# Attention and two layers on one core: reciprocals transposed and multiplied into a float32 output that layer 1 splits, and layer 2's mask and cubic constant made by ScalarE

## The chip, the core and the metric

The kernel runs on one core of a Trainium2 chip. TensorE (PE in the profile, its weight loads PEld) multiplies matrices into PSUM; VectorE (DVE), ScalarE (ACT) and GpSimd (POOL) work element by element; SyncE's queue (SP) issues the transfers. Each engine runs its own instructions in order and waits for others by semaphores. The metric is the time of one execution on the chip in microseconds, the median of several runs.

## The reference

Attention over 4 batches of 8 heads, 576 positions of 64 numbers, then two layers with different activations on its output of 2304 tokens by 512:

```python
q_rot, k_rot = rotate(q), rotate(k)
scores = (1 / sqrt(64)) * (q_rot @ k_rot.T)
attn = exp(scores - max(scores))
attn = attn / (sum(attn) + 1e-9)
x = attn @ v                                  # to 2304 x 512
h = x @ w_in                                  # layer 1, 512 x 2048
x = where(h > 0, h, exp(min(h, 0)) - 1) @ w_out
h = x @ w_in2                                 # layer 2
out = (h - tanh(h)) @ w_out2
```

## The kernel before

**Attention.** The heads come in 16 pairs (`p`). A pair has nine items (line 180): blocks `u` of 128 query rows, `u` = 0 to 3 once for each head (`h` = 0, 1), and a last item with the remaining 64 rows of both heads (`h` = None). The main loop goes over the 144 items and for each item `i` writes out work of several items, so that the engines overlap: the maximum of item `i` (`emit_max`, DVE), copies from PSUM that were left over (`flush`), the scores of item `i+1` (`emit_s`, PE), the exponentials of `i` with their row sums `den` (`emit_exp`, ACT), the normalisation of `i-1` (`emit_norm`: 1e-9 is added and the reciprocal taken on DVE, and POOL multiplies the exponentials `a` by it), the transposes of item `i-D` with `D = 4` (`emit_t`, PE, into `pt` and, for the 64 columns left of both heads, `pr`), and parts of the product with `v` (`emit_pv`, PE, into `o`). `flush` copies `pt` and `pr` to `aT` and `aTr`, two in five on DVE and three on ACT. `manual_schedule` keeps the order in which this is written on every engine.

The output `o` stays in PSUM until ACT has cast it to the float32r tile `xh` and, an item later, DVE has subtracted that from it into `xl` (lines 265 to 276): the layers multiply with such split numbers, high part and rest. Rotation of the next pair's q and k (`prep`, five steps at the items that `sched` names) multiplies with the tables `tabs` (line 143, mostly POOL), adds (line 145, DVE), casts (line 148, ACT) and subtracts (line 153, DVE); `place` then sends the parts to `qa`, `qb` and `k` through SP's queue. The scale 1/8 comes in with the last two steps. One weight block in two pairs is converted (`conv_w`, on ACT, DVE and POOL).

**Layers.** A step is one block of 128 of the 2048 inner columns for one tile of 384 tokens: 4 groups of 4 blocks by 6 tiles, 96 steps a layer. Per step PE makes `h` from 12 matmuls (`emit_f1`, line 441) and, four steps later (`LAG`), multiplies the activations `g` into `y` (`emit_f2`, line 498 in layer 1, 500 in layer 2). Four PSUM buffers hold `y`; a layer 2 tile needs three, and after its fourth step they are added to `acc` by DVE (line 517) or, in the first group, copied by ACT (line 515). In layer 2 `emit_act` and `emit_dve` (lines 453 to 476) make `h - tanh(h)`: for large `h` as a subtraction, and where `u = h*h` is under 0.09 by a polynomial `(w + G1) * h * u`, taken over through a mask.

Of the kernel before, what the change touches and what calls it, by code (L numbers as in the profile page):

```python
# [24 lines left out]
def attention_elu_tanhshrink(ctx: ExitStack, tc: tile.TileContext, qk, v, w1i, w1o, w2i, w2o, tab, out):  # L25
# [76 lines left out]
    with ExitStack() as actx:  # L102
# [17 lines left out]
        def load_qk(p, x):  # L120
            if p == 1 and x == 0:
                t = p3.tile([128, 2, S], F32, tag="a", name="t0")
            else:
                t = (p1, p2)[x].tile([128, 2, S], F32, tag=f"t{x}", name=f"t{x}")
# [8 lines left out]
        def prep(p, x, i):  # L133
            t = t_t[p, x]
            mul = SCALE if p > 0 and x == 0 else 1.0
            if i < 2:
# [4 lines left out]
                else:  # L141
                    eng = nc.vector if p < 2 and i == 1 else nc.gpsimd
                    eng.tensor_tensor(out=t[:, i, :], in0=t[:, i, :], in1=tabs[:, i, :], op=ALU.mult)  # L143
# [470 lines left out]
```

## Time and profile before

| | us |
|---|---|
| median of the runs (lowest, highest) | 1145.89 (1145.56, 1146.97) |
| the profiled execution | 1145.03 |
| its span in the profile | 1143.2 |
| PE busy | 1100.3 (96%) |
| DVE busy | 844.6 (74%) |
| POOL busy | 655.9 (57%) |
| ACT busy | 612.9 (54%) |

The busy times are averages over stages with different limits, so the table by stretch has to be read beside them. A busy PE isn't PE at its peak, since matmuls overlap and their ends are modelled. A row of the groups gives the line, engine, operation, what is written from what, shapes and count, then the busy time and the mean of one, then the engine's idle time before them and what ended it. A row of waits names who waited for whom. The chain of waits is followed back from the last instruction to what released each.

### The profile page before, as it was taken

What the parts mean: (1) busy time and instruction counts of PE and PEld (TensorE: products, weight loads), DVE (VectorE), ACT (ScalarE), POOL (GpSimd) and SP (SyncE); (2) the same over time, 40 slices, a digit from 0 to 9 for tenths busy, and PEclk for the clock granted to TensorE, in tenths of its full rate; (3) what the DMA queues carried; (4) which work ended last, traced back from release to release, by engine and by line L of the source; (5) the groups of instructions that cost most, each with busy time, mean ns of one, the idle gap of its engine ahead of it and who ended that gap; (6) DMA issues with size and microseconds to landing.
All of it is one profiled execution on the core that took longest, in us unless ns stands there. A gap on an engine that the chain in (4) does not pass through costs nothing.

```text
span 1143.2 us, 18404 instructions
## 1 busy us (share of the span) xinstructions
PE 1100.3 (96%) x6656; PEld 982.2 (86%) x6656; DVE 844.6 (74%) x1477; ACT 612.9 (54%) x1383; POOL 655.9 (57%) x585
## 2 busy tenths in 40 slices
PE   2899999999999999999999999999999999999998
PEld 2677776777789999999999999988999888999997
DVE  6998889888744334545544566898899999999775
ACT  3677777767634433333333343657766565655553
POOL 3877787778433333333333555866666566666553
PEclk9999999999999999999999999999999999999999
DMA  7767776766211111111111111011111111110102
GB/s 235 192 191 193 200 178 189 205 189 176 71 38 38 37 56 38 37 53 41 38 37 57 37 38 53 22 38 56 38 38 37 38 47 47 38 38 1 56 31 81
DMA packets 29627, 91.96 MB, mean 80 GB/s; under 512 B 4192, under 2 KB 4192, under 8 KB 29536
## 3 DMA queue, kind: packets, MB, share of 16 engines
q1 hardware_dynamic: 29536, 90.78, 27.6%
q8 instruction: 53, 0.87, 0.3%
q14 instruction: 38, 0.31, 0.1%
HBM read 57.74 MB, written 4.72 MB: 55 GB/s over the span
## 4 chain that ended last, share of the span: by engine, by line
PE 72%; DVE 21%; POOL 2%; ACT 2%; issue 1%; DMA 1%; SPq 1%; DVEq 0%; ACTq 0%
PE h L441 28%; PE y L498 17%; PE y L500 11%; PE o L326 6%; PE s L208 5%; PE pt L294 4%; DVE nm L217 3%; DVE f L476 3%; DVE w L475 2%; DVE f L84 2%; DVE aT L261 2%; DVE f L80 1%; DVE acc L517 1%; DVE hl L153 1%; DVE mask L474 1%
## 5 line engine op out<-in xcount | busy, mean ns | idle before, releaser
L441 PE MATMUL h<-xh,w 128*128 128x384 f32 x1536 | 424.1, 337 | 0.0
L483 POOL TENSOR_TENSOR g<-f,g 128x384 fp32r<-128x384 f32 x192 | 215.6, 1124 | 240.3 <-ACT g L482 240.2
L441 PEld LDWEIGHTS h<-xh,w 128*128 128x128 f32 x1536 | 281.7, 188 | 4.4
L441 PE MATMUL h<-xl,w 128*128 128x384 f32 x768 | 258.2, 336 | 0.0
L500 PE MATMUL y<-w,g 128*128 128x512 f32 x864 | 219.2, 399 | 7.7 <-DVE acc L517 4.6
L498 PE MATMUL y<-g,w 128*128 128x384 f32 x1152 | 215.2, 336 | 0.0
L498 PEld LDWEIGHTS y<-g,w 128*128 128x128 f32 x1152 | 201.1, 188 | 0.0
L500 PEld LDWEIGHTS y<-w,g 128*128 128x128 f32 x864 | 161.8, 189 | 40.0 <-DVE acc L517 5.7
L247 POOL TENSOR_SCALAR a<-a,r 128x576 f32<-128x576 f32 x144 | 132.2, 931 | 67.6 <-DVE r L244 49.9
L482 ACT CAST g<-f 128x384 fp32r<-128x384 f32 x192 | 99.3, 517 | 133.3 <-PE y L498 94.6
L468 DVE TENSOR_SCALAR f<-f 128x384 f32<-128x384 f32 x96 | 39.2, 408 | 147.9 <-ACT f L450 147.9
L441 PEld LDWEIGHTS h<-xl,w 128*128 128x128 f32 x768 | 144.6, 188 | 4.2
L458 POOL TENSOR_TENSOR q<-q,u 128x384 f32<-128x384 f32 x96 | 110.5, 1151 | 55.7 <-ACT q L457 55.5
L97 POOL TENSOR_TENSOR w<-f,w 128x512 fp32r<-128x512 f32 x64 | 87.9, 1374 | 90.7 <-ACT w L96 90.3
L217 DVE TENSOR_REDUCE nm<-s 128x1 f32<-128x576 f32 x144 | 108.0, 750 | 33.9 <-PE s L208 33.0
L231 ACT ACTIVATE a<-s,nm 128x576 f32<-128x576 f32 x144 | 107.5, 747 | 40.4 <-DVE nm L217 31.9
L450 ACT ACTIVATE f<-h 128x384 f32<-128x384 f32 x96 | 47.3, 492 | 147.8 <-PE h L441 141.0
L517 DVE TENSOR_TENSOR acc<-y,acc 128x384 f32<-128x384 f32 (+1 forms) x126 | 72.8, 611 | 47.1 <-PE y L498 40.8
L476 DVE COPY_PREDICATED f<-mask,w 128x384 f32<-128x384 uint8 x96 | 101.4, 1056 | 3.3
L143 POOL TENSOR_TENSOR t<-t,tabs 128x576 f32<-128x576 f32 x59 | 88.2, 1496 | 18.9 <-DMA t<-in_qk 15.8
L294 PE MATMUL pt<-ident,a 128*128 128x128 f32 x576 | 89.4, 278 | 3.9 <-ACT aT L263 2.7
L456 ACT ACTIVATE u<-h 128x384 f32<-128x384 f32 x96 | 47.3, 492 | 83.3 <-PE h L441 82.9
(56 smaller groups left out, 1498.7 us busy)
## 6 DMA issues: line engine op xcount, KB each, us to landing
k<-hl SPq DMA_DIRECT2D x64, 288.0 KB, 4.6
t<-in_qk SPq DMA_DIRECT2D x30, 576.0 KB, 4.9
raw<-in_w1i SPq DMA_DIRECT2D x16, 512.0 KB, 3.7
raw<-in_w1o SPq DMA_DIRECT2D x16, 512.0 KB, 3.6
raw<-in_w2i SPq DMA_DIRECT2D x16, 512.0 KB, 3.7
raw<-in_w2o SPq DMA_DIRECT2D x16, 512.0 KB, 3.6
v<-in_v SPq DMA_DIRECT2D x16, 288.0 KB, 5.0
qa<-hl SPq DMA_DIRECT2D x32, 144.0 KB, 2.3
```

The costliest lines, as they stand in the source:

```text
L143: eng.tensor_tensor(out=t[:, i, :], in0=t[:, i, :], in1=tabs[:, i, :], op=ALU.mult)
L217: nc.vector.tensor_reduce(out=nm, in_=s_t[i][:, :, 0:288], axis=AX.XY, op=ALU.max, negate=True)
L231: nc.scalar.activation(out=a.rearrange("p (x c) -> p x c", x=2), in_=s[:, :, 0:288], func=AF.Exp, bias=nm_t.pop(i), scale=1.0, accum_out=den,)
L247: nc.gpsimd.tensor_scalar(out=a, in0=a, scalar1=r[:, x:x + 1], scalar2=1.0, op0=ALU.mult, op1=ALU.mult)
L294: nc.tensor.transpose(pt[:, c, :], a[:, h or 0, c0:c0 + 128], ident)
L441: nc.tensor.matmul(out=hp, lhsT=w[:, wp, ws], rhs=x[:, c, xs], start=(m == 0), stop=(m == 3 * KC - 1))
L458: nc.gpsimd.tensor_tensor(out=q, in0=q, in1=u, op=ALU.mult)
L476: nc.vector.copy_predicated(f, mask, w)
L482: nc.scalar.copy(out=g[:, 0, :], in_=f)
L483: nc.gpsimd.tensor_tensor(out=g[:, 1, :], in0=f, in1=g[:, 0, :].bitcast(F32), op=ALU.subtract)
L498: nc.tensor.matmul(out=y_t[e][:, 0:NB], lhsT=w[:, wp, es], rhs=gt[:, gp, :], start=st, stop=sp)
L500: nc.tensor.matmul(out=y_t[e], lhsT=gt[:, gp, es], rhs=w[:, wp, :], start=st, stop=sp)
```

## The change

In attention the exponentials are no longer normalised before the transposes. `emit_recip` adds 1e-9 column by column and writes the reciprocals 128 columns wide (64 for each head, or 128 for the last item) into `r`; PE transposes `r` beside the rest `pr`, and `aTr` takes both in one copy. When `o` is complete, `flush_o` multiplies it on DVE by the transposed reciprocals into `xa`, a float32 tile that later serves as the layers' `acc`. `split_x` casts and subtracts a chunk of it (ACT and POOL) into `x_t`, one tile of split numbers per token tile: the first token tile in the last eight items of attention, the others in the first 20 steps of layer 1. The scale comes from a scaled table `tabq` that POOL makes at the start; the last rotation step goes to POOL for all pairs but the first. `D` is 2, and q is loaded two items earlier.

In layer 2 ACT makes the mask, `relu(0.09 - u)`, as float32 and reads as nonzero through a bitcast, and adds the constant `G1`; its copy of `h` goes away. POOL multiplies by `u`, DVE by `h` from PSUM.

```diff
+    def split_x(t, c):
+        a = xa[:, NTOK * c + NB * t:NTOK * c + NB * t + NB]
+        x = x_t[t]
+        nc.scalar.copy(out=x[:, 0, c, :], in_=a)
+        nc.gpsimd.tensor_tensor(out=x[:, 1, c, :], in0=a, in1=x[:, 0, c, :].bitcast(F32), op=ALU.subtract)
...
-                nc.vector.scalar_tensor_tensor(
-                    out=hl[:, 1, :], in0=t[:, 0, :], scalar=mul, in1=hl[:, 0, :].bitcast(F32),
-                    op0=ALU.mult, op1=ALU.subtract,
+                eng = nc.vector if p == 0 else nc.gpsimd
+                eng.tensor_tensor(
+                    out=hl[:, 1, :], in0=t[:, 0, :], in1=hl[:, 0, :].bitcast(F32), op=ALU.subtract
                 )
...
-            r = sm.tile([128, 2], F32, tag="r", name="r")
-            nc.vector.tensor_scalar_add(den, den, 1e-9)
-            nc.vector.reciprocal(out=r[:, 0:nh], in_=den)
+            r = r_t[p, u] = sm.tile([128, 128], F32, tag="r", name="r")
             for x in range(nh):
-                a = a_t[p, u][:, x, :]
-                nc.gpsimd.tensor_scalar(
-                    out=a, in0=a, scalar1=r[:, x:x + 1], scalar2=1.0, op0=ALU.mult, op1=ALU.mult
-                )
-
+                nc.vector.tensor_scalar_add(den[:, x:x + 1], den[:, x:x + 1], 1e-9)
+            nc.vector.reciprocal(
+                out=r.rearrange("p (h d) -> p h d", h=nh), in_=den.unsqueeze(2).broadcast_to([128, nh, 128 // nh])
+            )
...
-            for x0, hp, o, n in late_l:
-                nc.vector.tensor_tensor(
-                    out=xl[:, hp, x0:x0 + n], in0=o[:, 0:n], in1=xh[:, hp, x0:x0 + n].bitcast(F32),
-                    op=ALU.subtract,
-                )
-            late_l.clear()
-            for p, grp, o, n in late_x:
+
+        def flush_o():
+            for p, grp, o, aTr, n in late_o:
                 b, hp = divmod(p, 4)
-                x0 = b * S + 256 * grp
-                nc.scalar.copy(out=xh[:, hp, x0:x0 + n], in_=o[:, 0:n])
-                late_l.append((x0, hp, o, n))
-            late_x.clear()
+                x0 = NTOK * hp + b * S + 256 * grp
+                for sl, r in ((slice(0, 128), aTr[:, 1, :]),) if grp < 2 else (
+                        (slice(0, 64), aTr[0:64, 0, 64:128]), (slice(64, 128), aTr[64:128, 0, 128:192])):
+                    nc.vector.tensor_tensor(out=xa[sl, x0:x0 + n], in0=o[sl, 0:n], in1=r, op=ALU.mult)
+            late_o.clear()
...
+                nc.tensor.transpose(pr[:, 64:192], r_t.pop((p, u)), ident)
+                evac(aTr[:, 0, :], pr[:, 0:192])
...
+                nc.tensor.transpose(pr[:, 128:256], r_t.pop((p, u)), ident)
+                evac(aTr[:, :, q0:q0 + 128], pr[:, 0:256].rearrange("p (x c) -> p x c", x=2))
...
-        D = 4
+        D = 2
...
+            nc.gpsimd.tensor_scalar(out=tabq, in0=tabs, scalar1=SCALE, scalar2=1.0, op0=ALU.mult, op1=ALU.mult)
...
-                    emit_norm(i - 1)
+                    emit_recip(i - 1)
+                flush_o()
...
+                if n - 8 <= i < n and (i - n) % 2 == 0:
+                    split_x(0, (i - n + 8) // 2)
...
         nc.scalar.activation(out=u, in_=h, func=AF.Square)
-        nc.scalar.copy(out=q, in_=h)
-        nc.gpsimd.tensor_tensor(out=q, in0=q, in1=u, op=ALU.mult)
         nc.scalar.activation(out=w, in_=u, func=AF.Square, scale=S1, bias=b1)
+        nc.scalar.activation(out=w, in_=w, func=AF.Identity, bias=g1)
+        nc.gpsimd.tensor_tensor(out=w, in0=w, in1=u, op=ALU.mult)
         nc.scalar.activation(out=f, in_=h, func=AF.Tanh)
-        f_t[i] = (f, u, w, q)
+        mask = tmp.tile([128, NB], F32, tag="mask", name="mask")
+        nc.scalar.activation(out=mask, in_=u, func=AF.Relu, scale=-1.0, bias=us)
+        f_t[i] = (f, mask, w)
...
             nc.vector.tensor_tensor(out=f, in0=h, in1=f, op=ALU.subtract)
-            nc.vector.tensor_scalar(out=mask, in0=u, scalar1=U_SMALL, scalar2=None, op0=ALU.is_lt)
-            nc.vector.scalar_tensor_tensor(out=w, in0=w, scalar=G1, in1=q, op0=ALU.add, op1=ALU.mult)
-            nc.vector.copy_predicated(f, mask, w)
+            nc.vector.tensor_tensor(out=w, in0=h, in1=w, op=ALU.mult)
+            nc.vector.copy_predicated(f, mask.bitcast(U32), w)
...
+            if i < NJ * (NT - 1):
+                split_x(i // NJ + 1, i % NJ)
```

How the instructions stand on PE after the last scores of attention, before (`pt` and `pr` are transposes, `o` the product with `v`, `h` the first matmuls of layer 1), the first eleven rows, after which two more groups of four transposes come:

```order
L294 MATMUL pt<-ident,a 128x128 x4
L308 MATMUL pr<-ident,a 128x128
L294 MATMUL pt<-ident,a 128x128 x4
L326 MATMUL o<-aT,v 64x256 x6
L294 MATMUL pt<-ident,a 128x128 x4
L308 MATMUL pr<-ident,a 128x128
L441 MATMUL h<-xh,w_0_413 128x384
L441 MATMUL h<-xl,w_0_413 128x384
L441 MATMUL h<-xh,w_0_413 128x384
L294 MATMUL pt<-ident,a 128x128 x4
L326 MATMUL o<-aT,v 64x256 x2
```

and now, the first eleven rows, after which no group of four comes:

```order
L294 MATMUL pt<-ident,a 128x128 x4
L309 MATMUL pr<-ident,a 128x128
L310 MATMUL pr<-ident,r 128x128
L294 MATMUL pt<-ident,a 128x128 x4
L328 MATMUL o<-aT,v 64x256 x2
L328 MATMUL o<-aTr,v 64x256 x2
L294 MATMUL pt<-ident,a 128x128 x4
L309 MATMUL pr<-ident,a 128x128
L310 MATMUL pr<-ident,r 128x128
L451 MATMUL h<-x_68,w_0_443 128x384 x3
L294 MATMUL pt<-ident,a_4203 128x128 x4
```

Six groups of four transposes have become four, and each `pr` of two heads is followed by the transpose of its reciprocals `r`.

On DVE in layer 2, two steps with a part of a weight's conversion (`f<-raw`) between them, before:

```order
L473 TENSOR_TENSOR f<-h,f 128x384
L474 TENSOR_SCALAR mask<-u 128x384
L475 SCALAR_TENSOR_TENSOR w<-w,q 128x384
L476 COPY_PREDICATED f<-mask,w 128x384
L79 TENSOR_SCALAR f<-f 128x512
L80 TENSOR_SCALAR f<-f 128x512
L84 SCALAR_TENSOR_TENSOR f<-raw,f 128x512
L473 TENSOR_TENSOR f<-h,f 128x384
```

and now:

```order
L485 TENSOR_TENSOR f<-h,f 128x384
L486 TENSOR_TENSOR w<-h,w 128x384
L487 COPY_PREDICATED f<-mask,w 128x384
L85 TENSOR_SCALAR f<-f 128x512
L86 TENSOR_SCALAR f<-f 128x512
L90 SCALAR_TENSOR_TENSOR f<-raw,f 128x512
L485 TENSOR_TENSOR f<-h,f 128x384
```

The comparison that wrote the mask is gone, and the product reads `h`.

On ACT in layer 2, one step and the beginning of the next, before:

```order
L482 CAST g<-f 128x384
L456 ACTIVATE u<-h 128x384
L457 COPY q<-h 128x384
L459 ACTIVATE w<-u,b_4329 128x384
L460 ACTIVATE f<-h 128x384
L96 CAST w_1_9510<-f 128x512
```

and now:

```order
L493 CAST g<-f 128x384
L467 ACTIVATE u<-h 128x384
L468 ACTIVATE w<-u,b_4311 128x384
L469 ACTIVATE w<-w,g_4313 128x384
L471 ACTIVATE f<-h 128x384
L473 ACTIVATE mask<-u,us 128x384
L83 ACTIVATE f<-raw 128x512
```

In place of the copy `q<-h` stand an addition to `w` and, after `f`, the mask.

## Rows read from the trace of the kernel before

**Rows 1.** Table by stretch: length, busy us (instructions) of PE, PEld, DVE, ACT, POOL, PEclk, DMA
```profile
0.00:38.50 38.50, 15.52 (x72) 12.30 (x74) 27.27 (x40) 15.13 (x33) 16.31 (x19) 0.96 0.79 232
38.50:296.50 258.00, 250.30 (x2038) 185.05 (x2034) 229.38 (x476) 184.39 (x459) 202.42 (x186) 1.00 0.69 187
...
325.00:734.50 409.50, 409.50 (x2362) 409.50 (x2360) 212.32 (x407) 159.05 (x322) 171.95 (x154) 1.00 0.14 43
734.50:1143.20 408.70, 397.26 (x1957) 356.12 (x1956) 361.23 (x523) 238.76 (x530) 254.63 (x215) 0.99 0.13 41
```

**Rows 2.** Waits of PE, 734.5 to 1143.2: total us, times, longest
```profile
PE y L500 <- DVE acc L517: 4.6, 2, 2.3
PE y L500 <- ACT acc L515: 3.1, 1, 3.1
```

**Rows 3.** Chain that ended last, a piece in layer 2: start us, us, what
```profile
963.90 2.93 PE y L500 x6
```

**Rows 4.** Table by stretch, 3.4 us after the first wait (columns as in 1)
```profile
772.60:776.00 3.40, 3.40 (x11) 2.92 (x10) 1.98 (x4) 3.40 (x8) 2.69 (x3) 0.50 0.35 136
```

**Rows 5.** Groups by line, 734.5 to 1143.2: count | busy us, mean ns | idle before
```profile
L475 DVE SCALAR_TENSOR_TENSOR w<-w,q 128x384 f32<-128x384 f32 x93 | 76.9, 827 | 6.4 <-POOL q L458 6.4
...
L459 ACT ACTIVATE w<-u,b 128x384 f32<-128x384 f32 x92 | 57.9, 630 | 0.0
L473 DVE TENSOR_TENSOR f<-h,f 128x384 f32<-128x384 f32 x93 | 51.2, 550 | 26.9 <-ACT f L460 26.7
...
L474 DVE TENSOR_SCALAR mask<-u 128x384 uint8<-128x384 f32 x93 | 48.2, 519 | 0.0
...
L457 ACT COPY q<-h 128x384 f32<-128x384 f32 x92 | 43.7, 475 | 0.0
```

**Rows 6.** Chain that ended last, in attention: start us, us, what
```profile
136.40 0.44 PE pt L294 x4
136.84 0.11 PE pr L308
...
138.12 0.26 PE pr L301 x4
138.38 1.45 PE o L326 x12
```

**Rows 7.** Timeline: start us, us, engine, line, operation, count [idle before]
```profile
7.82 1.86 POOL L143 TENSOR_TENSOR t<-t,tabs 128x576 f32<-128x576 f32 x1 [6.51 <-DMA t<-in_qk]
...
10.40 1.76 DVE L145 TENSOR_TENSOR t<-t 128x576 f32<-128x576 f32 x1
...
157.43 1.27 DVE L243 TENSOR_SCALAR den<-den 128x2 f32<-128x2 f32 x1
...
159.93 0.60 PE L294 MATMUL pt<-ident,a 128*128 128x128 f32 x4
...
161.02 0.33 PE L308 MATMUL pr<-ident,a 128*128 128x128 f32 x1 [0.49 <-DVE aT L261]
```

**Rows 8.** Groups by line, 38.5 to 296.5 us (columns as in 5)
```profile
L247 POOL TENSOR_SCALAR a<-a,r 128x576 f32<-128x576 f32 x126 | 117.5, 946 | 41.5 <-DVE r L244 23.8 <-PE s L208 7.7 <-ACT a L231 2.5
...
L243 DVE TENSOR_SCALAR den<-den 128x2 f32<-128x2 f32 x56 | 25.0, 446 | 0.0
...
L153 DVE SCALAR_TENSOR_TENSOR hl<-t,hl 128x576 fp32r<-128x576 f32 x28 | 23.4, 834 | 1.1
...
L266 DVE TENSOR_TENSOR xl<-o,xh 128x256 fp32r<-128x256 f32 x28 | 11.6, 414 | 0.0
...
L244 DVE RECIPROCAL r<-den 128x2 f32<-128x2 f32 x56 | 9.3, 166 | 1.9
...
L266 DVE TENSOR_TENSOR xl<-o,xh 128x64 fp32r<-128x64 f32 x14 | 3.0, 214 | 0.0
...
L244 DVE RECIPROCAL r<-den 128x1 f32<-128x1 f32 x14 | 2.3, 164 | 0.5
L243 DVE TENSOR_SCALAR den<-den 128x1 f32<-128x1 f32 x14 | 2.0, 143 | 0.0
```

More of the change, by code (lines that the diff above doesn't have):

```diff
@@ L113, in attention_elu_tanhshrink @@
         tabs = acst.tile([128, 2, S], F32, name="tabs")
+        tabq = acst.tile([128, 2, S], F32, name="tabq")
         zero = acst.tile([128, 64], F32, name="zero")
@@ L120, in load_qk @@
         def load_qk(p, x):
[L121 to L124, printed above, removed]
+            t = p2.tile([128, 2, S], F32, tag=f"t{x}", name=f"t{x}")
             nc.sync.dma_start(out=t, in_=qk[p, :, 2 * x:2 * x + 2, :])
@@ L142, in prep @@
                     eng = nc.vector if p < 2 and i == 1 else nc.gpsimd
[L143 removed]
+                    tb = (tabq, tabs)[x]
+                    eng.tensor_tensor(out=t[:, i, :], in0=t[:, i, :], in1=tb[:, i, :], op=ALU.mult)
             elif i == 2:
@@ L147, in prep @@
                 hl_t[p, x] = p1.tile([128, 2, S], F32R, tag=f"hl{x}", name=f"hl{x}")
-                nc.scalar.mul(hl_t[p, x][:, 0, :], t[:, 0, :], mul)
+                nc.scalar.copy(out=hl_t[p, x][:, 0, :], in_=t[:, 0, :])
             else:
@@ L306, in emit_t @@
             if h == 1:
-                pr = ps_t.tile([128, 4, 128], F32, tag="pt", name="pr")
-                nc.tensor.transpose(pr[:, 0, :], a.rearrange("p h s -> p (h s)")[:, 512:640], ident)
-                evac(aTr[:, q0:q0 + 128], pr[:, 0, :])
+                pr = ps_t.tile([128, 512], F32, tag="pt", name="pr")
+                nc.tensor.transpose(pr[:, 0:128], a.rearrange("p h s -> p (h s)")[:, 512:640], ident)
+                nc.tensor.transpose(pr[:, 128:256], r_t.pop((p, u)), ident)
+                evac(aTr[:, :, q0:q0 + 128], pr[:, 0:256].rearrange("p (x c) -> p x c", x=2))
         o_t = {}
@@ L343, in attention_elu_tanhshrink @@
             for x in range(2):
-                when = [i0 + o for o in ((-8, -6, -4, -3, -2, -1), (-7, -2, 0, 2, 3, 4))[x]]
+                when = [i0 + o for o in ((-10, -6, -4, -3, -2, -1), (-7, -2, 0, 2, 3, 4))[x]]
                 if p in early:
@@ L353, in attention_elu_tanhshrink @@
             for x in range(2):
-                t = t_t[0, x] = (p1, p2)[x].tile([128, 2, S], F32, tag=f"t{x}", name=f"t{x}")
+                t = t_t[0, x] = p2.tile([128, 2, S], F32, tag=f"t{x}", name=f"t{x}")
                 for i in range(2):
@@ L372, in attention_elu_tanhshrink @@
             pend = []
+            nw = list(range(len(first_w)))[::-1]
             emit_s(0)
@@ L382, in attention_elu_tanhshrink @@
                         f(*arg)
-                if r == 0 and p % 2 == 0 and p // 2 < len(first_w):
-                    load_w(first_w[p // 2])
+                if i == 1 or i % (2 * NI) == 12:
+                    load_w(first_w[nw.pop()]) if nw else None
                 if i < n:
@@ L425, in attention_elu_tanhshrink @@
     ps_y = ctx.enter_context(tc.tile_pool(name="ps_y", bufs=4, space=PSUM))
-    acc = fcst.tile([128, KC * NTOK], F32, name="acc")
+    for t in range(1, NT):
+        x_t[t] = fcst.tile([128, 2, KC, NB], F32R, name=f"x{t}")
+    acc = xa
     b1 = fcst.tile([128, 1], F32, name="b1")
+    us = fcst.tile([128, 1], F32, name="us")
+    g1 = fcst.tile([128, 1], F32, name="g1")
     h_t, f_t, g_t, y_t = {}, {}, {}, {}
@@ L438, in emit_f1 @@
             ws = slice(128 * c, 128 * c + 128)
-            xs = slice(NB * t, NB * t + NB)
-            for wp, x in ((0, xh), (0, xl), (1, xh)):
-                nc.tensor.matmul(out=hp, lhsT=w[:, wp, ws], rhs=x[:, c, xs], start=(m == 0), stop=(m == 3 * KC - 1))
+            for wp, xp in ((0, 0), (0, 1), (1, 0)):
+                nc.tensor.matmul(
+                    out=hp, lhsT=w[:, wp, ws], rhs=x_t[t][:, xp, c, :], start=(m == 0), stop=(m == 3 * KC - 1)
+                )
                 m += 1
@@ L520, in emit_acc @@
                 if l == 0:
-                    xs = slice(NB * t, NB * t + NB)
-                    nc.scalar.copy(out=xh[:, e, xs], in_=a)
-                    nc.gpsimd.tensor_tensor(
-                        out=xl[:, e, xs], in0=a, in1=xh[:, e, xs].bitcast(F32), op=ALU.subtract
-                    )
+                    split_x(t, e)
                 else:
```

34 lines of the change are left out of this document (16 added, 18 removed).

## Prediction

> **What bounds the kernel now.** I read first the table of busy time by stretch [rows 1]. It has three stages: attention to about 325 us, layer 1 to 734.5 us, layer 2 to the end. In layer 1 TensorE (PE) is busy for all of its 409.5 us and nothing else comes near, so no edit there can move the end unless it makes PE wait. In layer 2 PE is idle for 11.4 of 408.7 us while VectorE (DVE) is busy for 361.2. In the main part of attention PE is busy for 250.3 of 258 us and DVE for 229.4: both near their limits, PE the nearer.
>
> Second, who PE waits for in layer 2 [rows 2]: 7.7 us in three waits, always for the additions or copies that empty an output tile `y`. [...] Behind a second wait, which ends at 963.90, six matmuls of `y` take 2.93 us in the chain [rows 3], half a microsecond each, where a step of 408.7/96 = 4.3 us holds nine of them and twelve of `h`. The stalls of layer 2 together cost 7.7 + 2 x 1.7 = 11.1 us.
>
> **Layer 2's edits.** Per step (96 steps) DVE loses the comparison that makes the mask (0.519), and its product changes from a two-operation one on two SBUF tiles (0.827) to a product of the PSUM tile `h` with `w`, which has the form of the subtraction (0.550) [rows 5]. That is 0.52 + 0.28 = 0.80 us a step, 77 us in all; DVE goes from 361 to about 284 of 409. ScalarE (ACT) loses the copy (0.475) and gains two operations of the form of its second square (0.630): +0.79 us a step, 75 us, so it goes from 239 to about 314. GpSimd (POOL) keeps one product a step. PE's three waits are short against what DVE gets back: two to three steps give 1.6 to 2.4 us, about one wait. I take 10 of the 11.1 us as won; the bounds are 7 and 11.1. The copy through the mask stays at its price: its mask is four bytes wide now, and no row shows that form.
>
> So 0.52 us on DVE is dearer here than 0.63 on ACT, since it is DVE that PE waits for. [...]
>
> **Attention: PE.** Each of the 80 blocks of rows has one more 128x128 transpose, of its reciprocals. Four transposes take 0.44 us in the chain and the single one of the rest 0.11 [rows 6]: 64 x 0.11 = 7.0 us. The 16 at the end of a pair follow small 64x64 products (0.26 for that group) and change the array's shape twice; between 0.11 and 0.26 I take 0.2, since they have a change of shape in common: 3.2 us. Together 10.2 us, all of it on the path, since PE has no other free time than its waits. If those 16 cost 0.11 it is 8.8; if 0.26, 11.2.
>
> **Attention: what feeds PE.** Waits of PE in the main part come to 7.7 us [rows 1]. At 161.02 it waits 0.49 us for a copy out of PSUM by DVE; on DVE, 3.6 us earlier, an addition on 128x2 numbers takes 1.27 us [rows 7]. Such additions take 0.446 on average, those on 128x1 only 0.143 [rows 8]. Per pair DVE changes as follows. Additions: 4 x 0.446 + 0.143 become 9 x 0.143, -0.64. Two subtractions `hl` go to POOL: -2 x 0.834 = -1.67. The reciprocals grow from 2 columns to 128, and no row has such a one. From one column to two it goes from 164 to 166 ns, 2 ns a column, hence 0.166 + 126 x 0.002 = 0.42 (my value, as it is the row of the same operation; with the 1.04 ns a column of the subtractions `xl`, 414 against 214 ns for 256 against 64 columns, it would be 0.30): 5 x 0.42 - 0.83 = +1.27. Three subtractions `xl` become two products of 256 columns and two of 64: +0.21. Two copies become wider by 128 columns: +0.27. In all -0.56 us a pair (-1.2 with the lower value), from 229.4/14 = 16.4. ACT loses three casts and gets wider copies. POOL loses nine multiplications of 0.946, which stood between the exponentials and the transposes, and gets two subtractions. So all that feed PE become lighter, and I take 7 us of the stalls as won. The new product waits, on DVE, for the last PE product of a tile; behind it stand the next maximum and the copies. It is issued after the reciprocal, when PE is nearly through, and I cost it at nothing. Without that cover it waits up to half of a part like the 1.45 us of [rows 6], three times a pair, 2.2 us, and DVE has 18.4 - 15.8 = 2.6 free (a pair takes 258/14 = 18.4).
>
> So the main part and the ends give +10.2 - 7 = +3 us. Its bounds are -4 and +10.2. The upper one: no stall goes. The lower: a stall costs more than it shows. At 161.02 the transpose before began 0.77 us earlier, three of 0.11 after 159.93, and 0.66 of it is over the pace where 0.49 is shown; by that 7.7 us is 10, and shorter waits that no view lists come on top, for which I add 4.
>
> **Attention: both ends.** The transposes follow their scores by two items, not four. After the last scores of before stand six groups of four transposes, now four; one part of the product with `v` also moves ahead (1.45 [rows 6]). That is 2 x 0.44 + 0.11 + 1.45 = 2.4 us of PE work moved from the end of attention to the start, where PE is busy for 15.5 of 38.5 us [rows 1]. I take 2; the bounds are 0 and 3. At the start POOL now first makes the scaled table, 1152 columns, at most twice the 0.946 us of a multiplication of 576, ahead of its first product, which began at 7.82 and ended at 9.68; the sum that needs it began at 10.40 [rows 7]. Of 1.9 us 0.7 is free. I add 0.5 us, between 0 and 1.2.
>
> The splits of `x` for layer 1 (an ACT cast and a POOL subtraction a tile and chunk) move from the attention loop to the first 20 steps of layer 1. Their cover is a stage in which ACT is busy for 39% and POOL for 42% [rows 1]. It is tightest in the first four steps, which have no `y` on PE: POOL has about six subtractions there. Cost nothing; without that cover 1 to 2 us, once.
>
> **The sum.** The profiled execution took 1145.0 us (1143.2 and 1.8 around it), 0.9 under the median of the runs, 1145.9. 1145.9 - 10 + 3 - 2 + 0.5 = 1137.4, so 1137.
>
> **Rivals.** (a) Attention gives back all its waits while layer 2 wins all 11: 1145.9 - 11 - 4 - 2 + 0.5 = 1129. For it: POOL no longer stands between exponentials and transposes, and DVE gets lighter. Against it: the conversion of weights on DVE stays, and so does the chain through maxima, exponentials and copies.
>
> (b) No wait of attention goes, since they come from the order of maxima, exponentials and copies: 1145.9 - 10 + 10.2 - 2 + 0.5 = 1144.6, no change that counts.
>
> [...]
>
> (d) Layer 2's gain is eaten: ACT, with two more operations and the copies of the first round, empties `y` late, or the four-byte mask makes the copy through it longer. With a wait like the longest of before (3.1) in each of the first round's six tiles, at 2 to 3 us, the gain of 10 becomes a loss of 2 to 8: 1149 to 1155. It decides when ACT reaches the 409 us of the stage, and 314 isn't that.
>
> **Chances.** My sum (1130 to 1143.6) 48%; (a) 18%; (b) 13%; (c) 10%; (d) 6%; 5% for slower ways that I don't see. Faster by over 0.2% (2.3 us, about what a measurement of this kernel can tell) are the first two and a little of (b): 0.68; within it 0.12; slower 0.20. The range goes from 1125 to 1150: it leaves out (c), most of (d) and the lowest of (a).
>
> **What would show it.** Layer 2: PE waits under 2 us, no stretch at half clock, DVE near 284 and ACT near 314 us; if PE still waits for `y` with DVE light, that step is wrong. [...] A pair at about 18.6 us against 18.4: above 19, the waits stayed; below 18.1, (a). Layer 1 shows no wait of PE. I am wrong if PE's waits in attention grow although DVE, ACT and POOL get lighter.

## The result and the profile after

The changed kernel takes 1154.21 us (median of 4 runs, 1153.57 to 1155.29), the kernel before 1145.72 us beside it. The ratio is 1.0074, with a 95% interval of 1.0057 to 1.0092: slower, where 1137 us and faster were forecast. The profiled execution took 1154.66 us, with a span of 1152.9.

The table of busy time by stretch, with the columns of [rows 1], of the changed kernel: start, main part of attention, layer 1, layer 2.

```profile
0.00:38.50 38.50, 16.62 (x94) 13.71 (x96) 25.51 (x41) 15.42 (x35) 13.23 (x14) 1.00 0.79 226
38.50:296.50 258.00, 244.40 (x1974) 179.99 (x1973) 236.54 (x484) 165.28 (x392) 121.61 (x88) 1.00 0.66 180
342.00:756.40 414.40, 414.40 (x2356) 414.40 (x2355) 218.71 (x404) 170.06 (x345) 192.82 (x175) 1.00 0.14 43
756.40:1152.90 396.50, 392.53 (x1957) 352.83 (x1955) 291.98 (x427) 311.81 (x622) 245.46 (x214) 1.00 0.13 42
```

In the main part PE now idles 13.6 us of 258 (7.7 before), and DVE, which was to become lighter, has gone from 229.4 to 236.5. In layer 2 PE idles 4.0 us where it idled 11.4, nearly all of it at the very end. The granted clock is 1.00 in every stretch: the stretches at 0.50 [rows 4] are gone.

To see where the 9.7 us of the two spans come from, I read four instants out of each trace: the first and the last product for scores, the first product of `y` in layer 1, and the first in layer 2. These are starts of single instructions. "Layer 1" is from its first `y` to layer 2's first; "layer 2" from there to the last `y`. All in us; the runs below are described in the next section.

| kernel | time (median) | first score | last score | first `y` | layer 1 | layer 2 |
|---|---|---|---|---|---|---|
| before | 1145.7 | 12.2 | 313.2 | 334.5 | 400.0 | 404.6 |
| changed | 1154.2 | 13.6 | 331.6 | 350.6 | 405.8 | 392.3 |
| l2_alone | 1139.0 | 11.9 | 313.6 | 335.0 | 405.8 | 391.9 |
| attn_alone | 1160.2 | 13.7 | 329.6 | 348.6 | 400.0 | 404.5 |
| narrow | 1140.4 | 13.4 | 317.4 | 336.4 | 405.8 | 392.3 |
| narrow_40 | 1145.6 | 13.1 | 323.2 | 342.2 | 405.8 | 391.9 |
| narrow_dve_g | 1142.7 | 13.0 | 324.2 | 343.2 | 400.0 | 393.1 |
| double | 1215.8 | 13.3 | 394.3 | 413.3 | 405.8 | 392.3 |
| narrow_nort | 1134.1 | 13.1 | 311.2 | 329.7 | 405.8 | 391.9 |
| narrow_d4 | 1153.1 | 13.4 | 327.4 | 349.3 | 405.8 | 391.9 |
| narrow_g | 1136.1 | 13.6 | 317.8 | 336.8 | 400.0 | 393.6 |
| l2_g | 1134.0 | 12.6 | 313.5 | 334.8 | 400.0 | 393.4 |
| l2_g_d2 | 1217.3 | 12.1 | 393.3 | 412.8 | 400.0 | 393.6 |

So attention costs 16.1 us more (first `y`), layer 1 costs 5.8 more, and layer 2 gives 12.3 back. The middle one nobody had on the list: PE waits for nothing in layer 1, before or after.

Layer 2 went as forecast. Groups by line of the changed kernel in that stage, as in [rows 5], and the only wait of PE there:

```profile
L487 DVE COPY_PREDICATED f<-mask,w 128x384 f32<-128x384 uint32 x93 | 88.7, 953 | 9.6
L486 DVE TENSOR_TENSOR w<-h,w 128x384 f32<-128x384 f32 x92 | 51.1, 555 | 19.1 <-POOL w L470 19.1
L469 ACT ACTIVATE w<-w,g 128x384 f32<-128x384 f32 x92 | 56.8, 617 | 3.0
L473 ACT ACTIVATE mask<-u,us 128x384 f32<-128x384 f32 x92 | 55.7, 605 | 0.0
```

```profile
PE y L511 <- ACT xa L526: 0.2, 1, 0.2
```

The product takes 0.555 us (0.550 was assumed), ScalarE's two operations 0.617 and 0.605 (0.630 assumed), DVE is at 292 and ACT at 312 us (284 and 314 forecast). The copy through the mask, which the forecast left at its price, went from 1.053 us with the one-byte mask of before to 0.953. The three waits of [rows 2] have shrunk to one of 0.2.

Attention did not. The groups by line of DVE, 38.5 to 296.5 us, to hold against [rows 8]:

```profile
L249 DVE RECIPROCAL r<-den 128x128 f32<-128x128 f32 x67 | 63.9, 953 | 2.3
L264 DVE COPY aT<-pt 128x512 f32<-128x512 f32 (+1 forms) x52 | 31.9, 614 | 0.0
L275 DVE TENSOR_TENSOR xa<-o,aTr 128x256 f32<-128x256 f32 (+1 forms) x52 | 15.2, 292 | 2.7 <-PE o L328 2.6
L248 DVE TENSOR_SCALAR den<-den 128x1 f32<-128x1 f32 x118 | 12.6, 144 | 0.2
```

The 128-column reciprocal takes 0.953 us. It was priced at 0.42; by the forecast's other terms DVE reaches the 18.4 us of a pair at 0.94 a reciprocal (16.4 - 0.64 - 1.67 + 0.48 - 0.83 + 5 x 0.94). What it does is to be seen in the chain that ended last, here less than half of a pair (start us, us, what; each piece was released by the one above it; `nm` are the maxima, `den` the additions, `f` a weight's conversion):

```profile
195.88 0.60 DVE aT L264
196.48 0.13 DVE den L248 x2
196.61 0.02 issue
196.64 0.95 DVE r L249
197.59 0.61 DVE nm L221
198.20 0.07 DVE den L248
198.27 0.02 issue
198.29 0.95 DVE r L249
199.24 0.28 DVE xa L275
199.53 0.59 DVE f L94
200.12 0.67 DVE nm L221
200.78 0.61 DVE aT L264
201.39 0.04 issue
201.44 0.33 PE pr L301 x4
201.77 0.26 PE pr L303
202.03 1.45 PE o L328 x12
203.47 0.74 PE s L212 x4
```

For 5.5 us the end of the program hangs on DVE alone, one instruction behind the other: two copies out of PSUM, two maxima, a weight conversion and two reciprocals. At 201.44 PE has waited 0.74 us, since both buffers for transposes are full and the last copy stands behind all this. The waits of PE in the main part, summed by what was waited for (us in total, times, longest):

```profile
PE pr L301 <- DVE aT L264: 7.5, 13, 1.5
PE s L212 <- ACT a L235: 4.3, 19, 0.3
```

Thirteen times in some thirteen pairs, so in each. A pair takes 19.6 us on average where it took 18.4. But the pairs are not alike. From one such group of transposes (`pr` of the last item) to the next it is mostly 19.1 and 20.2 us in turn, and the waits before them are short and long in turn (PE: start us, us, what, idle before):

```profile
101.89 0.33 PE L301 MATMUL pr<-ident,a 64*64 64x64 f32 x4 [0.25 <-DVE aT L264]
122.07 0.33 PE L301 MATMUL pr<-ident,a 64*64 64x64 f32 x4 [0.74 <-DVE aT L264]
141.12 0.33 PE L301 MATMUL pr<-ident,a 64*64 64x64 f32 x4 [0.26 <-DVE aT L264]
```

The long waits stand in the pairs in which DVE converts a weight: its last conversion instruction begins at 80.84, 120.07 and 160.21 us, and none lies near 101.89 or 141.12. The piece of the chain above is of such a pair; in the next one, without a conversion, the stretch on DVE alone is 4.9 us. In the whole main part the reciprocal makes up 10.4% of the chain.

### The profile page after: what moved, and what is told of

Read it like the earlier page. It is cut to its first block, busy times and chain, and to the rows that moved or that the text cites. A ratio compares the mean times of both kernels' runs of the same rounds, so it can differ in the third digit from the quotient of the medians.

```text
span 1152.9 us, 18403 instructions
## 1 busy us (share of the span) xinstructions
PE 1111.3 (96%) x6736; PEld 992.7 (86%) x6736; DVE 808.5 (70%) x1433; ACT 689.3 (60%) x1455; POOL 579.9 (50%) x496
## 4 chain that ended last, share of the span: by engine, by line
PE 82%; DVE 13%; ACT 1%; issue 1%; DMA 1%; SPq 0%; POOL 0%; POOLq 0%; ACTq 0%
PE h L451 35%; PE y L509 18%; PE y L511 17%; PE o L328 6%; DVE nm L221 5%; PE s L212 4%; DVE r L249 3%; DVE aT L264 2%; PE pt L294 1%; DVE t L149 1%; DVE f L85 1%; ACT a L235 1%; DVE f L94 1%; PE pr L309 0%; ACT aT L266 0%
## 5 line engine op out<-in xcount | busy, mean ns | idle before, releaser
L451 PE MATMUL h<-x,w 128*128 128x384 f32 x2304 | 434.2, 336 | 0.0
L451 PEld LDWEIGHTS h<-x,w 128*128 128x128 f32 x2304 | 407.1, 188 | 7.6
L470 POOL TENSOR_TENSOR w<-w,u 128x384 f32<-128x384 f32 x96 | 106.5, 1110 | 99.6 <-ACT w L469 99.6
L103 POOL TENSOR_TENSOR w<-f,w 128x512 fp32r<-128x512 f32 x64 | 82.8, 1293 | 92.1 <-ACT w L102 86.5
L528 DVE TENSOR_TENSOR xa<-y,xa 128x384 f32<-128x384 f32 (+1 forms) x126 | 74.0, 612 | 47.2 <-PE y L509 42.0
L485 DVE TENSOR_TENSOR f<-h,f 128x384 f32<-128x384 f32 x96 | 53.2, 554 | 68.9 <-ACT f L471 68.3
L487 DVE COPY_PREDICATED f<-mask,w 128x384 f32<-128x384 uint32 x96 | 91.5, 953 | 9.9
L158 POOL TENSOR_TENSOR hl<-t,hl 128x576 fp32r<-128x576 f32 x30 | 42.3, 1413 | 100.5 <-ACT hl L152 100.5
L328 PE MATMUL o<-aT,v 128*64 128x256 f32 (+1 forms) x768 | 80.1, 337 | 0.0
L55 POOL TENSOR_TENSOR x<-xa,x 128x384 fp32r<-128x384 f32 x48 | 52.1, 1100 | 53.3 <-ACT x L54 53.1
```

What stands on the lines that cost most here:

```text
L103: nc.gpsimd.tensor_tensor(out=w[:, 1, :], in0=f, in1=w[:, 0, :].bitcast(F32), op=ALU.subtract)
L328: nc.tensor.matmul(out=o[sl, 0:n], lhsT=w, rhs=m, start=(c == 0), stop=(c == 4))
L451: nc.tensor.matmul(out=hp, lhsT=w[:, wp, ws], rhs=x_t[t][:, xp, c, :], start=(m == 0), stop=(m == 3 * KC - 1))
L470: nc.gpsimd.tensor_tensor(out=w, in0=w, in1=u, op=ALU.mult)
L487: nc.vector.copy_predicated(f, mask.bitcast(U32), w)
```

## The experiments

**Which part costs what: l2_alone and attn_alone.** The first is the kernel before with layer 2's edits, the second the changed kernel without them:

```diff
-        nc.scalar.copy(out=q, in_=h)
-        nc.gpsimd.tensor_tensor(out=q, in0=q, in1=u, op=ALU.mult)
+        nc.scalar.activation(out=w, in_=w, func=AF.Identity, bias=g1)
+        nc.gpsimd.tensor_tensor(out=w, in0=w, in1=u, op=ALU.mult)
...
+    us = fcst.tile([128, 1], F32, name="us")
+    g1 = fcst.tile([128, 1], F32, name="g1")
```

> The kernel before with layer 2's edits alone; attention and layer 1 are those of before. In the changed kernel layer 2 (last y of layer 1 to last y) took 12.2 us less than before, while layer 1 took 5.5 us more, because its matmuls follow each other at 176.1 ns against 173.6, without a wait. Theory: layer 2's gain stands by itself and the pace of layer 1's matmuls came with the attention part: 1145.7 - 12 = 1133.5 us, matmul pace in layer 1 still 173.6 ns. Rival: layer 1's slower pace comes with layer 2's code: 1139 us, pace 176.1 ns. Second rival: the gain of layer 2 needed the later start or other tiles of the changed kernel: over 1141 us.

> The changed kernel with layer 2's edits undone, so attention's change and the moved splits alone. Theory: attention's 16.1 us and layer 1's 5.5 us both belong to this part: 1145.7 + 21.6 = 1167 us, layer 1's pace 176.1 ns, the waits of layer 2 back (PE idle near 11 us there). Rival: layer 1's pace belongs to layer 2's code: 1162 us and 173.6 ns.

l2_alone took 1138.99 us (ratio 0.9945, 0.9932 to 0.9957), attn_alone 1160.18 (1.0129, 1.0115 to 1.0143). In both the rival holds, not my theory: layer 1 takes 405.8 us in l2_alone, whose attention and layer 1 are word for word those of before, and 400.0 in attn_alone. So layer 2's edits, which execute nothing in layer 1 but two memsets of one column, slow layer 1 by 5.8 us.

**The width of the reciprocal: narrow and double.** In narrow, DVE makes the reciprocal on 1 or 2 columns and POOL widens it:

```diff
-            nc.vector.reciprocal(
-                out=r.rearrange("p (h d) -> p h d", h=nh), in_=den.unsqueeze(2).broadcast_to([128, nh, 128 // nh])
-            )
+            rs = sm.tile([128, 2], F32, tag="rs", name="rs")
+            nc.vector.reciprocal(out=rs[:, 0:nh], in_=den)
+            nc.gpsimd.tensor_copy(
+                out=r.rearrange("p (h d) -> p h d", h=nh),
+                in_=rs[:, 0:nh].unsqueeze(2).broadcast_to([128, nh, 128 // nh]),
+            )
```

In double the wide reciprocal stands there twice:

```diff
             nc.vector.reciprocal(
                 out=r.rearrange("p (h d) -> p h d", h=nh), in_=den.unsqueeze(2).broadcast_to([128, nh, 128 // nh])
             )
+            nc.vector.reciprocal(
+                out=r.rearrange("p (h d) -> p h d", h=nh), in_=den.unsqueeze(2).broadcast_to([128, nh, 128 // nh])
+            )
```

> The changed kernel, but the reciprocal is made on 1 or 2 columns as before (0.166 us in the trace of before) and POOL copies it out to 128 columns; all else, the 80 transposes of it too, stays. Theory W (the 128-column reciprocal at 0.953 us, five a pair, delays the maxima, products and copies behind it on DVE): DVE loses 5 x 0.79 = 3.9 us a pair, the pair goes from 19.6 back to 18.4 to 18.8, 13 to 19 us less: 1135 to 1141. Rival T (the 80 transposes and the product that waits for the last PE product of a tile, at the head of DVE's queue, make the loss): pair stays over 19.3, 1150 to 1154. Middle: if POOL's copy makes the transposes of r late, PE shows a wait for it, and the gain is smaller.

> The changed kernel with every 128-column reciprocal made twice, one behind the other on DVE (80 more of 0.953 us = 76 us of DVE work). Theory W (the reciprocal lies on the path at its full length, since PE waits for what is queued behind it): 1154 + 76 = 1230 us, at least 1215. Rival T (DVE is only near its limit: 19.6 - 16.9 = 2.7 us a pair are free): 16 x (4.8 - 2.7) = 33 us more, about 1188.

narrow took 1140.39 us (0.9956, 0.9942 to 0.9970): 13.8 us less than the changed kernel, of which the first `y` shows 14.3. A pair takes 18.7 us, with a conversion or without. Theory W holds, and the 80 transposes and the waiting product, which are still there, are not the cause of these 14 us. The table by stretch and the waits of PE for narrow, 38.5 to 296.5 us:

```profile
38.50:296.50 258.00, 254.06 (x2080) 189.43 (x2080) 201.68 (x509) 173.69 (x414) 154.87 (x159) 1.00 0.68 184
```

```profile
PE s L212 <- ACT a L235: 3.1, 14, 0.2
PE pr L313 <- POOL r L251: 0.3, 1, 0.3
```

DVE is down to 201.7 us, the wait for its copy is gone, and in the main part no reciprocal is left in the chain that ended last, 90% of which is now PE. double took 1215.79 us (1.0616, 1.0602 to 1.0631), between my two figures: 62 us more for 76 us of DVE work, with a granted clock that fell (mean 0.979 of the execution, 0.92 in the main part, where PE idled 40.2 of 258 us).

**Price or rule: narrow_40 and narrow_dve_g.** The forecast had priced the wide reciprocal at 0.42 us and held that it cost nothing until DVE reached the pace of a pair. narrow_40 gives it that price: as narrow, but on 40 columns, of which POOL copies one a head out to 128.

```diff
-            rs = sm.tile([128, 2], F32, tag="rs", name="rs")
-            nc.vector.reciprocal(out=rs[:, 0:nh], in_=den)
+            rs = sm.tile([128, 40], F32, tag="rs", name="rs")
+            rv = rs.rearrange("p (h d) -> p h d", h=nh)
+            nc.vector.reciprocal(out=rv, in_=den.unsqueeze(2).broadcast_to([128, nh, 40 // nh]))
```

narrow_dve_g is narrow with the widening copy on DVE (and with the two constant tiles moved, as in narrow_g below):

```diff
-            nc.gpsimd.tensor_copy(
+            nc.vector.tensor_copy(
```

> The run narrow, but DVE makes the reciprocal on 40 columns and POOL copies it out to 128. If the reciprocal grows evenly from 166 ns at 2 columns to 953 ns at 128 (6.2 ns a column), it takes 0.40 us, which is about what the forecast gave the wide one (0.42). Theory (the forecast's threshold: below the point where DVE reaches the pace of a pair, its work costs nothing): within 1.5 us of narrow, 1139 to 1142 us. Rival (each microsecond of DVE costs in proportion, 14.3 us for 0.79 us more a reciprocal): 14.3 x 0.24/0.79 = 4.3 us more, 1144.7 us.

> The run narrow_g, but DVE itself copies the narrow reciprocal out to 128 columns, so that r costs DVE 0.166 us and a copy that I put at 0.2 to 0.3 us: about the 0.42 us that the forecast gave the wide reciprocal. Theory (DVE delays TensorE only when r takes much longer than that; the forecast's step was wrong in the price alone): within 2 us of narrow_g, 1135 to 1138 us. Rival (any work on DVE between a maximum and the copies behind it costs time at full length): 80 x 0.2 to 0.3 = 16 to 24 us more, 1152 to 1160 us; half of that lies between.

The 40 columns took 0.403 us. The run took 1145.64 us (1.0001, 0.9991 to 1.0010), 5.2 more than narrow; by the traces the first `y` came 5.9 us later. So the rival, 4.3 us, is the nearer, and the rule has fallen: 0.24 us more on DVE, five times a pair, with DVE at 214.7 of 258 us, costs time. In narrow_dve_g the copy took longer than I had put it, 0.611 us, so `r` cost 0.78 together; 1142.68 us (0.9977, 0.9967 to 0.9986), 6.6 more than narrow_g. The groups by line of the two, and their largest wait of PE (38.5 to 296.5 us), first narrow_40:

```profile
L251 DVE RECIPROCAL rs<-den 128x40 f32<-128x40 f32 x68 | 27.4, 403 | 2.3
```

```profile
PE pr L305 <- DVE aT L268: 4.4, 7, 1.1
```

then narrow_dve_g:

```profile
L251 DVE COPY r<-rs 128x128 f32<-128x128 f32 x67 | 40.9, 611 | 2.3
```

```profile
PE pr L304 <- DVE aT L267: 4.6, 7, 1.3
```

The wait for the last copy of a pair is back in both, in every second pair (7 in 13.5). In narrow_40:

```profile
196.28 0.33 PE L305 MATMUL pr<-ident,a 64*64 64x64 f32 x4 [0.57 <-DVE aT L268]
215.00 0.33 PE L305 MATMUL pr<-ident,a 64*64 64x64 f32 x4
234.35 0.33 PE L305 MATMUL pr<-ident,a 64*64 64x64 f32 x4 [0.58 <-DVE aT L268]
```

Again these are the pairs with a conversion, whose last instruction on DVE begins at 193.91 and 231.98 us: a pair with one mostly takes 19.36 us, one without 18.73, as in narrow. No run takes the conversion away, so that it is the cause is read from the trace and not tested. At 0.953 us the wait came in each pair. So the cost does not grow evenly: 0, 5.9, 6.4, 14.3 and 77 us of attention for 0.17, 0.40, 0.78, 0.95 and 1.9 us a block of rows (the third in two instructions and held against narrow_g, the last with the fallen clock).

**The transposes: narrow_nort.** The two lines that transpose `r` are left out, and the copies out of PSUM read other numbers at the same width.

```diff
-                nc.tensor.transpose(pr[:, 128:256], r_t.pop((p, u)), ident)
-                evac(aTr[:, :, q0:q0 + 128], pr[:, 0:256].rearrange("p (x c) -> p x c", x=2))
+                r_t.pop((p, u))
+                evac(aTr[:, :, q0:q0 + 128], pr[:, 0:128].unsqueeze(1).broadcast_to([128, 2, 128]))
```

> The run narrow without the 80 transposes of the reciprocals; the copies out of PSUM keep their width, and the product is made with other numbers, so the normalisation is left out. Theory (the forecast's price: 64 x 0.11 + 16 x 0.2 = 10.2 us, all on TensorE's path): last score 10 us earlier, 1130 us. Rival (what feeds TensorE sets the pace in narrow, so that the transposes fill waits): under 3 us less, 1137 to 1140 us.

1134.07 us, 6.3 less than narrow: between the two. Their own length was as forecast. In the chain of the changed kernel above one takes 0.26 at the end of a pair, and elsewhere it is 0.11 (piece below, from the same chain). Without them PE idles 7.3 of 258 us where narrow has 3.9, so about 4 of their 10 us fill waits that would be there without them.

```profile
205.65 0.33 PE pr L309
205.98 0.11 PE pr L310
```

**The distance of two: narrow_d4 and l2_g_d2.** One line each, the first in narrow, the second in l2_g (below), whose attention is that of before:

```diff
-        D = 2
+        D = 4
```

```diff
-        D = 4
+        D = 2
```

> The run narrow with the transposes four items behind their scores again, as in the kernel before, in place of two. Theory (the forecast's term for the ends): 2 us of PE work go back to the end of attention: 1140.4 + 2 = 1142.4 us, last score to first steady matmul of layer 1 13.0 us in place of 10.7. Rival (the distance of two costs the main part waits, since exponential, reciprocal and its copy must be ready two items later): main part shorter by more than 2 us, 1140 us or less.

> The run l2_g (attention as before, layer 2's edits, g in its old place) with the transposes two items behind their scores in place of four, which is the part of the change at the ends, alone. Theory (the forecast's term: 2 us of PE work leave the end, nothing else moves): 1134 - 2.5 = 1131.5 us. Rival (POOL's two multiplications of 0.946 us a pair of items stand between exponential and transposes, and at a distance of two PE waits for them in every item): over 1140 us.

Both theories fall. narrow_d4 took 1153.07 us (1.0067, 1.0054 to 1.0079), 12.7 more than narrow. From the last score to the first `y` it is 21.9 us against 19.0, the 2.9 that the term for the ends speaks of; the other 10 us are in the main part, whose pairs take 19.6 us on average, where narrow has 18.7. l2_g_d2 took 1217.33 us (1.0631, 1.0609 to 1.0652), 83 more than l2_g, by its rival's mechanism and far more of it, again with a fallen clock (0.93 in the main part). Its largest wait of PE, 38.5 to 296.5 us:

```profile
PE pt L294 <- POOL a L247: 42.5, 36, 2.1
```

Here the transposes wait for POOL's multiplications. So the distance of two is no matter of the ends alone. It can't be had with the old normalisation, and the new one without it loses 10 us in the main part. Why a pair is longer at four is open: in narrow_d4 PE waits for three things with 1.8 to 5.5 us each, and no run takes them apart. The chain gives a lead: 21.4% of it in the main part are transfers of `k` (`DMA k<-hl`, some 4 us each), of which narrow's chain has none.

**Layer 1: an address.** l2_alone left little that could reach layer 1. The two new tiles of one column stand in front of the tile `g`, each takes 32 bytes in the program's layout, and so `g`, whose halves PE reads as the operand `rhs` of `y` in layer 1 (128x384 in the trace, where the loaded weights are 128x128), begins at byte 202976 of each partition in place of 202912. The expected pace is layer 1's length over its 2304 matmuls: 400.0 us is 173.6 ns, 405.8 is 176.1. before_pad is the kernel before with 64 unused bytes there:

```diff
     b1 = fcst.tile([128, 1], F32, name="b1")
+    pad = fcst.tile([128, 16], F32, name="pad")
...
+        nc.vector.memset(pad, 0.0)
```

narrow_g is narrow with the two tiles in a pool of their own behind the others:

```diff
     tmp3 = ctx.enter_context(tc.tile_pool(name="tmp3", bufs=3))
+    fcst2 = ctx.enter_context(tc.tile_pool(name="fcst2", bufs=1))
...
-    us = fcst.tile([128, 1], F32, name="us")
-    g1 = fcst.tile([128, 1], F32, name="g1")
+    us = fcst2.tile([128, 1], F32, name="us")
+    g1 = fcst2.tile([128, 1], F32, name="g1")
```

> The kernel before with one unused SBUF tile of 64 bytes a partition in front of the tile g, which is all that this changes for layer 1 (and one memset): g moves from byte 202912 to 202976 of each partition, where the changed kernel has it too. Theory A (the address of g sets the pace of the matmuls that read it): layer 1's pace goes from 173.6 to 176.1 ns, its length from 400.0 to 405.8 us: 1145 + 5.8 = 1151 us. Rival B (something else in layer 2's edits, other instructions or the order of instructions in memory, sets it): 1145 us, 173.6 ns.

> The run narrow with the two new constant tiles placed behind the others, so that g stands at byte 202912 again, as in the kernel before. Theory A: layer 1 takes 400.0 us, 1140.4 - 5.8 = 1134.6 us. Rival B: layer 1 stays at 405.8 us, 1140.4 us.

before_pad took 1151.68 us (1.0053, 1.0039 to 1.0066), with 405.8 us in layer 1: theory A, to 0.1 us. narrow_g took 1136.05 (0.9916, 0.9903 to 0.9930), with 400.0 us there; its layer 2 is 1.3 us longer. But in all these runs the tile `f`, on which the other engines work, had moved along with `g`. pad_f puts 64 bytes in front of `f` alone, and pad_g 64 in front of `g` and 192 more in front of `f` (one execution each, as in the two runs behind them; layer 1 is read from the trace). The edit of pad_g, without the lines that set the new tiles to zero; pad_f has the last two lines alone, with 16 in place of 48:

```diff
+    pad = fcst.tile([128, 16], F32, name="pad")
...
+    fpad = ctx.enter_context(tc.tile_pool(name="fpad", bufs=1))
+    pad2 = fpad.tile([128, 48], F32, name="pad2")
```

> The kernel before with an unused tile of 64 bytes a partition between the tiles of layer 2 and f: f moves from byte 222112 to 222176, g stays at 202912. In before_pad both had moved by 64. TensorE reads g; VectorE, ScalarE and GpSimd read and write f. If the matmuls' pace follows the address that TensorE reads, it stays at 173.6 ns and layer 1 at 400.0 us; if it follows where the other engines work, 176.1 ns and 405.8 us.

> The kernel before with unused tiles of 64 bytes in front of g and of 192 bytes in front of f: g moves by 64 to byte 202976, f by 256, so that its place within 256 bytes is as before. If the pace follows g's address, it is 176.1 ns and layer 1 takes 405.8 us; if f's, 173.6 ns and 400.0 us.

pad_f (1145.93 us): 400.0 us in layer 1. pad_g (1150.94): 405.8. So it is the address of `g`, not that of `f`. But ScalarE and GpSimd write `g` where PE reads it, and no run moves the one without the other; whether the reading or the writing counts is not shown. Groups by line of PE from 380 to 700 us, for pad_f and then pad_g:

```profile
L500 PE MATMUL y<-g,w 128*128 128x384 f32 x924 | 172.6, 336 | 0.0
L443 PE MATMUL h<-xh,w 128*128 128x384 f32 x614 | 168.4, 334 | 0.0
```

```profile
L501 PE MATMUL y<-g,w 128*128 128x384 f32 x906 | 172.3, 339 | 0.0
L444 PE MATMUL h<-xh,w 128*128 128x384 f32 x608 | 168.1, 337 | 0.0
```

Three ns more for the mean matmul, and fewer of them in the same 320 us. The matmuls of `h`, which read `x` and not `g`, are slower too (334 and 337 ns). By the starts, one by one, in the traces of before and of the changed kernel, whose `g` stands where pad_g has it, the first seven steps of each twelve of `h`, right behind those of `y`, go from 174.4 to 177.4 ns, and the last five stay at 173.3. Two more runs, with 8 and 32 in place of 16 in before_pad's edit, ask which places are good:

> The kernel before with an unused tile of 32 bytes a partition in front of g: g at byte 202944, a multiple of 64 and not of 128. The pace was 173.6 ns at 202912 (32 above a multiple of 128) and 176.1 ns at 202976 (96 above one). Theory 1 (the crossing of 64-byte borders costs): the pace is 173.6 ns or less. Theory 2 (it depends on the place within 128 or 256 bytes in another way): anything between 173.6 and 176.1 ns, or above.

> The kernel before with an unused tile of 128 bytes a partition in front of g: g at byte 203040, again 32 above a multiple of 128, but 32 above a multiple of 256 where before it was 160. If the place within 128 bytes decides, the pace of layer 1's matmuls is 173.6 ns and the layer takes 400.0 us; if the place within 256 bytes decides, another pace.

With 32 bytes (1146.88 us) layer 1 takes 401.3 us, with 128 (1150.34) it takes 403.8. The same groups, with 32 bytes and then with 128:

```profile
L499 PE MATMUL y<-g,w 128*128 128x384 f32 x917 | 171.1, 336 | 0.0
L442 PE MATMUL h<-xh,w 128*128 128x384 f32 x615 | 169.7, 337 | 0.0
```

```profile
L499 PE MATMUL y<-g,w 128*128 128x384 f32 x915 | 174.3, 340 | 0.0
L442 PE MATMUL h<-xh,w 128*128 128x384 f32 x609 | 167.2, 335 | 0.0
```

With 32 bytes only the matmuls of `h` are longer, which do not read `g`; with 128 it is those of `y` almost alone. So theory A holds for the layer's length, not in its words "the matmuls that read it". Neither the crossing of 64-byte borders nor the place within 128 bytes gives the order 400.0 (0), 401.3 (32), 405.8 (64), 403.8 (128). What in the address counts is open.

**The version that beats both: l2_g.** The edit of l2_alone, with the two new tiles behind the others by the edit of narrow_g; attention as before.

> The kernel before with layer 2's edits (the run l2_alone) and with the two new constant tiles placed behind the others, so that g stands at byte 202912 as before. Theory A (the address of g sets layer 1's pace): 400.0 us in layer 1, 1139.0 - 5.8 = 1133.2 us, up to 1134.5 if layer 2 is longer with g there, as it was by 1.2 us in narrow_g. Rival: 1139 us.

1134.04 us, ratio 0.9902 (0.9885 to 0.9918). Layer 2 keeps 11.2 us of gain and nothing is paid for it. narrow_g, with the whole change, a narrow reciprocal and `g` in its place, comes within about 2 us of that (1136.05).

## Why the prediction was wrong

**The step that failed** is the one on what feeds PE in attention, and it failed twice. First the price: "2 ns a column, hence 0.166 + 126 x 0.002 = 0.42". The reciprocal takes 0.166 us at 2 columns, 0.403 at 40 and 0.953 at 128, so 6.2 ns for each column between; from one column to two nothing of this shows. The bound from below, 0.30, came from a subtraction, and none was set from above. By the runs this costs 342.2 to 350.6 = 8.4 us, the difference between narrow_40 and the changed kernel.

Second the rule: that DVE's work costs nothing while DVE has "2.6 free" in a pair. With the price about as forecast (narrow_40; its widening on POOL, which the forecast does not have, cost PE 0.3 us of waits in narrow) attention is 342.2 - 334.5 = 7.7 us longer, not the 1.5 of the sum: 6.2 us missed. An average over all pairs hides two things. DVE's conversion of a weight falls into every second pair, and narrow_40 waits in those alone. And within a pair it does not see the 5.5 us in the chain above in which DVE is the path, with two of the five reciprocals in it. This gives no price: two reciprocals in each of 16 pairs, longer by 0.24 us in narrow_40 and by 0.79 in the changed kernel, would be 7.6 and 25 us, where 5.9 and 14.3 were measured against narrow. Part of the time only fills what DVE still had free; how much, the runs give only at the widths that were tried.

**The step that was not there** is layer 1. I wrote that no edit could move its end "unless it makes PE wait". PE waits for nothing, and 5.8 us were lost to the place of a tile. Nothing in the profile of before could have told the price; what could have been seen is that two new tiles in front of `g` move an operand of 1152 matmuls of that stage. Whether the reading or the writing of `g` counts no run tests: pad_f, which moves `f`, leaves layer 1 at 400.0 us, but `g` is written by ScalarE and GpSimd, and its writing moved with its reading.

**Layer 2**: right in mechanism and nearly in size. 10 of 11.1 us were forecast; l2_g shows 11.2, about the stated upper bound, and the changed kernel 12.3. The 1.1 between them go with the layout: layer 2 takes 391.9 to 392.3 us in all runs with the two new tiles in front of `g`, and 393.1 to 393.6 with them behind. The 11.1 is 7.7 us of waits and 2 x 1.7, and no run shows the 1.7 as a time: it is an estimate, half of 3.4 us. What the traces show is two stretches at a granted clock of 0.50 in layer 2 of before, 3.4 us each, from 772.60 [rows 4] and from 963.75 us, and none in the changed kernel. Rival (d) has no support: two operations of 0.61 us a step on ScalarE in place of a copy of 0.475 left PE one wait of 0.2 us.

**PE in attention**: 10.2 us for the transposes were about right as work (0.11 each, and 0.26 at the end of a pair where 0.2 was taken, so 11.2); as time narrow_nort shows 6.3.

**The ends**: from the last score to the first `y` 21.3 us became 19.0, -2.3 where -2 was forecast. At the start the first score came 1.4 us later (0.5 forecast, at most 1.2); the other runs with the new table lie from 0.8 to 1.5 later, those without it from 0.3 earlier to 0.7 later. The distance of two is worth more than its end, as narrow_d4 shows, but in narrow, where DVE is light, main part and ends together are what the sum said: the first `y` comes at 336.4, 1.9 us later, and 1.5 was forecast.

**Put together**, against the profiled 1145.0: attention 1.5 + 6.2 (rule) + 8.4 (price) = 16.1, layer 1 5.8, layer 2 -12.3; 1154.6, and the profiled execution took 1154.7. The three stages are cut from the two traces themselves, so that they add up is no proof; the split of the 16.1 rests on narrow_40.

**The mechanism** is that the reciprocal makes DVE the path. An average pace does not give its size. The forecast's terms put DVE at the 18.4 us of a pair with 0.94 us a reciprocal, so by its rule the measured 0.953 would have cost 16 x 5 x 0.013 = 1.0 us, next to nothing; against narrow 14.3 were measured. The 6.2 ns a column between 2 and 128 columns are six times the 1.04 ns a column of the subtractions in [rows 8], which had served for the bound from below.

## What to carry to other kernels

Price an operation at the width that it will have: two rows of one and two columns (2 ns apart) did not show the slope of 6.2 ns a column, and a bound from above must come from somewhere. Whether an engine's work costs time is read from the chain through one round of the loop, not from its busy share: DVE at 83% (214.7 of 258 us in narrow_40) delayed TensorE in a passage where it was the path, by 5.9 us against narrow. Work that comes in every second round has to be counted in its own round, not spread over two. And put small new tiles behind the operands of the matmuls, or compare the matmuls' pace before and after, since a moved operand can cost time without any wait, here 5.8 us.

## What the runs showed of the hardware

- Where the tile `g` begins 32, 64 or 128 bytes further on, the matmuls of layer 1 (384 columns, twelve that read `g` and twelve that read `x` in turn) follow each other 0.3, 1.4 or 1.0% more slowly (400.0 us become 401.3, 405.8 and 403.8), with no idle time of PE before them (0.0 in the rows from 380 to 700 us). The granted clock of layer 1 is 1.00 in before and, with `g` 64 bytes further on, in the changed kernel. Moving `f` by 64 bytes changes nothing (400.0, pad_f).
- A reciprocal on DVE takes 0.166, 0.403 and 0.953 us for 2, 40 and 128 columns (before, narrow_40, changed kernel).
- A copy that spreads one or two columns over 128 took 0.485 us on POOL (narrow) and 0.611 on DVE (narrow_dve_g), where a copy out of PSUM by DVE takes 0.681 with 512 columns and 0.414 with 256 (changed kernel). The POOL row of narrow, 38.5 to 296.5 us:

```profile
L251 POOL COPY r<-rs 128x128 f32<-128x128 f32 x70 | 33.9, 485 | 97.3 <-DVE rs L250 48.9 <-PE pt L297 38.0 <-PE s L212 10.0
```
